# Linear attention and two feed-forward layers on one core: the attention's normalisation moved to tokens on partitions, the first block's loads rebuilt, and a new model of the queues in the planner

## The chip, the cores and the metric

One core of one Trainium2 chip runs the whole program. Times are device microseconds (us). The kernel before takes 1663.95 us, the median of three runs (1659.26 to 1665.63).

## The reference

Everything is float32.

```
kv  = einsum('bhsd,bhse->bhde', k, v)          # 8 batches, 8 heads, 576 tokens, 64 wide
out = einsum('bhsd,bhde->bhse', q, kv)
x   = out / sqrt(mean(out*out, -1) + 1e-6) * g_norm      # per head; then 4608 tokens x 512
h = x @ w_in;   g = s * relu(h)**2 + b;   x = g @ w_out      # 512 -> 2048 -> 512
h = x @ w_in2;  g = h * cos(h);           out = g @ w_out2
```

The weights arrive as float64, so each tile of them is first converted: two 32-bit words are turned into one float32 by two ScalarE and four VectorE operations (function w_conv, lines 313 to 366).

## The kernel before

**How a product is computed.** A float32 matmul is either "native" (one instruction of two passes for each product, lines 672 and 518) or "split": each operand is kept as a rounded part and a remainder (hi, lo), and three single-pass products (hi hi, hi lo, lo hi) are summed in PSUM (lines 629 to 631 and 680). Splitting an operand costs one ScalarE copy and one VectorE subtraction.

**Stages.** The 4608 tokens are nine blocks of 512. Blocks 0 to 2 go through the first layer in 48 steps (a block has 16 slices f of the hidden width; step i is block i // 16, slice i % 16). Step i computes h (mm_h, line 621, twelve passes of 512 columns), activates it (act1, line 640) and adds to four accumulators (mm_o, line 665). In block 0 the steps that are in WHOLE, all 16, use the unsplit w_out and native matmuls (line 672); while block 1 runs, split_late (line 383) splits these w_out tiles for the later steps. Blocks 3 to 8 and the whole second layer are done afterwards in 80 pairs of slices with a Strassen-like scheme (mm_h2, line 809, act2, act1_pair, mm_o1). The trace has the first instruction of these pairs at 389 us.

**Attention.** attn_unit (line 538) makes x for one block and one pair of heads: four units for each block. Where a new batch begins, kv_unit (line 486) loads k and v as four rows per partition on 128 partitions (512 tokens, 1 KB packets) and the last 64 tokens as "tails" on 64 partitions (256 B packets), in four DMAs (lines 497 and 500; for blocks 2 and up from POOL's queue), and multiplies them in ten matmuls (line 518). q is brought with its width on partitions: in block 0 by four TensorE transposes (line 551), else by 128 B packets and a VectorE transpose (line 572). Then xps = kv.T q, 512 tokens along the free axis (line 582); the mean of squares over a head lies along partitions, so it is a matmul with a matrix of 1/64 (line 588 native in block 0; else the squares are split, lines 591 and 592, and two passes are made, lines 596 and 597). The inverse root is refined by one Newton step on 128x512 tiles: two ScalarE operations (602, 604) and three VectorE operations (606, 608, 610). For blocks 0 to 2 the result is split (532, 533); for the others it is stored to memory (615).

**Order.** The order on every engine is worked out beforehand by class Plan (lines 61 to 159). Each op has an engine, a cost and a due time; the planner runs a clock for each engine, takes the op that can start first, and among those within 0.1 us the one due first. SP, SUM (POOL's queue) and AQ (ScalarE's queue) are such engines too; after an op its users wait for AFTER (0.13 to 0.2 us for compute, 2.0, 4.5 and 3.0 us for the three queues). On the chip each engine runs its list in that order and waits where the model was too early. warm_up (line 904) adds 40 matmuls of the identity that fill TensorE where the plan finds nothing else.

**Block 0's loads** (load_block0, line 464): two w_in tiles go first on ScalarE's queue (line 319); SP takes k and v of the first head pair, both tails, q in 256 B packets (line 473), the constants (line 285), then the other head pairs and the other weights.

Of the kernel before, what the change touches and what calls it, by code (L numbers as in the profile page):

```python
# [10 lines left out]
F32 = mybir.dt.float32  # L11
# [29 lines left out]
FIRST_LOADS = {0: -39.6, 1: -38.7, 2: -37.6, 3: -36.8}  # L41
WARM = 40

WHOLE = range(16)
# [16 lines left out]
class Plan:  # L61
# [7 lines left out]
    AFTER = {"PE": 0.2, "DVE": 0.13, "ACT": 0.13, "POOL": 0.13, "SP": 2.0, "SUM": 4.5, "AQ": 3.0}  # L69
# [6 lines left out]
    def op(self, eng, cost, due, fn, w=(), p=(), r=(), keep=(), after=()):  # L76

# [25 lines left out]
    def run(self):  # L103
        engines = dict(self.START)
        ready = {e: [] for e in self.AFTER}
# [13 lines left out]
        def start(o):  # L119
            t = max(engines[o.eng], o.ready)  # L120
            for x in o.refs:
                if x.slots and x.t is None:
                    t = max(t, min(free_at(s) for s in x.slots))
            return t

        n = 0
        while n < len(self.ops):
# [13 lines left out]
            end = t + o.cost  # L141
            engines[o.eng] = end
# [7 lines left out]
            for x in o.refs:  # L150
                x.left -= 1
                x.end = max(x.end, end)
                if not x.left and x.slots:
                    hold(x.slot, x.end + self.AFTER[o.eng])
            for u in o.users:
                u.ready = max(u.ready, end + (0.0 if u.eng == o.eng == "PE" else self.AFTER[o.eng]))
# [6 lines left out]
def fused_kernel(  # L163
# [27 lines left out]
    R = S // P  # L191
    TAIL = S - R * P
# [62 lines left out]
    EARLY = {"kv_raw", *Q_RAW, *TAIL_, *KV_F, *QT, *QH, *QL}  # L255
# [14 lines left out]
    ones = cpool.tile([P, P], F32R, name="ones")  # L270
    nc.vector.memset(f32(ones), 0.0)
    for j in range(2):

        nc.vector.memset(f32(ones)[j * D:(j + 1) * D, j * D:(j + 1) * D], 1.0 / D)
# [4 lines left out]
    small = cpool.tile([P, 5], F32, name="small")  # L279
    g_sb, g_neg, s_sb, b_sb, spare = (small[:, i:i + 1] for i in range(5))  # L280
    g_ref, sb_ref = Ref(), Ref()

    def load_consts():
        for j in range(2):
            op("SP", 0.5, -39.5, lambda j=j: nc.sync.dma_start(
                out=g_sb[j * D:(j + 1) * D, :], in_=g_norm.rearrange("(p o) -> p o", o=1)), p=[g_ref])
        op("DVE", 0.1, -30, lambda: nc.vector.tensor_scalar(
            out=g_neg, in0=g_sb, scalar1=-1.0, scalar2=None, op0=ALU.mult), w=[g_ref])
        for t, src in ((s_sb, moe_s), (b_sb, moe_b)):
            op("SP", 0.5, -30, lambda t=t, src=src: nc.sync.dma_start(  # L290
# [22 lines left out]
    def w_conv(ph, kind, f, by, load_by=None, after=()):  # L313
# [5 lines left out]
        early = ph == 0 and kind == "i" and f < 2  # L319
        queue = nc.scalar if early else nc.sync  # L320
# [18 lines left out]
        op("AQ" if early else "SP", 1.0 if early else 1.5, by - 12 if load_by is None else load_by, load, w=[raw], after=after)  # L339

        op("ACT", 0.67, by - 6, lambda: nc.scalar.activation(t.t, w1().bitcast(F32), AF.Abs), w=[t], r=[raw])  # L341
        op("DVE", 0.43, by - 5, lambda: nc.vector.tensor_scalar(
            out=t.t, in0=t.t, scalar1=F64_HI, scalar2=F64_LO, op0=ALU.min, op1=ALU.max), w=[t])
        op("DVE", 0.43, by - 5, lambda: nc.vector.tensor_scalar(
            out=ti(), in0=ti(), scalar1=3, scalar2=0x3FFFFFFF, op0=ALU.logical_shift_left, op1=ALU.bitwise_and),
            w=[t])
        op("DVE", 0.69, by - 4.5, lambda: nc.vector.scalar_tensor_tensor(
# [3 lines left out]
        op("ACT", 0.67, by - 4.5, lambda: nc.scalar.activation(w0(), w0().bitcast(U32), AF.Copy, scale=2.0 ** -29),  # L351
           w=[raw])
        if ph == 0 and kind == "o" and f in WHOLE:

            op("DVE", 0.69, by - 3, lambda: nc.vector.tensor_tensor(out=w0(), in0=ti(), in1=w0(), op=ALU.add),
# [3 lines left out]
        op("DVE", 0.69, by - 3, lambda: nc.vector.tensor_tensor(out=ti(), in0=ti(), in1=w0(), op=ALU.add),  # L359
# [11 lines left out]
    def split_in(kind, f, t, by):  # L371

        hi = w_t[0, kind, f] = sref([(WO if kind == "o" else WI)[f]], F32R, (2, 512))
        op("ACT", 0.62, by - 1, lambda: nc.scalar.copy(hi.t[:, 0, :], t.t), w=[hi], r=[t])
# [89 lines left out]
    def load_block0():  # L464
# [17 lines left out]
        for hp in range(1, KC):  # L482
            load_kv(hp, -40 + hp)
            load_q(hp, -40 + hp)
# [545 lines left out]
```

## Time and profile before

| | |
|---|---|
| runs | 1665.63, 1659.26, 1663.95 us; median 1663.95 |
| profiled execution, from first to last instruction | 1660.2 us |
| what lies around that span | not given for the profiled execution; the median of the runs is 3.75 us above its span |
| TensorE busy | 1634.8 us (98%) |
| VectorE, ScalarE, GpSimd busy | 1136.9, 916.9, 86.3 us |
| weight loads on TensorE | 1424.3 us (86%) |
| mean granted TensorE clock | 0.996 of full speed |

TensorE is busy nearly all the time, so what counts is where it is not, and where what it does is a filler (line 910) or more passes than needed. A row of a window gives busy time (and instructions, x) of each engine, then the granted TensorE clock, the busy share of the DMA engines and what they moved in GB/s. In a timeline a row is: start, length, engine, line, operation, output <- input, shape, count, and in brackets the idle time before it with what ended that. Ends of matmuls are modelled: the time of a group is read from its start to the next start.

### The profile page before, as it was taken

The page shows a single profiled execution, that of the slowest core. Times are in us where ns is not written, and L with a number is a line of the kernel's source. Part 1 is how long each engine was busy: PE and PEld are TensorE (multiplying, and loading weights), DVE is VectorE, ACT ScalarE, POOL GpSimd, SP SyncE. Part 2 cuts the span into 40 slices and gives each one's busy share as a digit, 9 for nine tenths or more (in the row PEclk, how much of TensorE's full clock was granted, in tenths as well). Part 3 has the DMA queues.
Part 4 walks back from the last instruction along what each step waited for, and adds up shares of the span by engine and source line. Part 5 has one row for each costly group of instructions (what it writes and reads, how often), then busy time and mean ns, then how long its engine had stood idle before and what let it go on. Part 6 is the DMA issues. An engine that isn't in the chain of part 4 may idle for free.

```text
span 1660.2 us, 23829 instructions
## 1 busy us (share of the span) xinstructions
PE 1634.8 (98%) x8648; PEld 1424.3 (86%) x8648; DVE 1136.9 (68%) x1804; ACT 916.9 (55%) x1551; POOL 86.3 (5%) x142
## 2 busy tenths in 40 slices
PE   8999999999999999999999999999999999999999
PEld 6666776778989989988999998998998998988987
DVE  6897787785667767767346567567567577577564
ACT  6775765454556556556335455555555555455443
POOL 0012443300000000000000000000000000000000
PEclk9999999999999999999999999999999999999999
DMA  9733788944678777876565543443443444444431
GB/s 304 210 99 93 204 226 213 267 144 128 234 227 270 251 247 242 262 252 198 184 220 197 172 153 124 153 155 121 151 160 120 149 158 125 148 156 128 147 116 55
DMA packets 207446, 297.29 MB, mean 179 GB/s; under 512 B 89313, under 2 KB 134369, under 8 KB 207329
## 3 DMA queue, kind: packets, MB, share of 16 engines
q1 hardware_dynamic: 198848, 274.26, 53.1%
q0 software_dynamic: 7424, 20.46, 4.2%
q8 instruction: 69, 1.13, 0.3%
q10 hardware_dynamic: 1056, 1.05, 0.2%
q14 instruction: 49, 0.39, 0.1%
HBM read 232.79 MB, written 62.91 MB: 178 GB/s over the span
## 4 chain that ended last, share of the span: by engine, by line
PE 55%; DMA 1%; ACT 0%; issue 0%; DVE 0%; SPq 0%; ACTq 0%; DVEq 0%
PE h L823 25%; PE a L680 16%; PE h L680 8%; PE a L718 4%; PE h L718 2%; DMA w2i_d<-t 0%; DMA raw<-in_moe_w_out_dram 0%; DMA raw<-in_moe_w_in_dram 0%; ACT t L835 0%; ACT c L341 0%; ACT wi L896 0%; ACT wi L893 0%; DVE t L396 0%; ACT t L395 0%; ACT t L698 0%
## 5 line engine op out<-in xcount | busy, mean ns | idle before, releaser
L823 PE MATMUL h<-shared,wi 128*128 128x384 f32 x2256 | 466.9, 337 | 3.2 <-ACT t L835 3.2
L823 PEld LDWEIGHTS h<-shared,wi 128*128 128x128 f32 x2256 | 400.5, 188 | 15.8 <-ACT t L835 4.2
L680 PE MATMUL a<-wo,wi 128*128 128x512 f32 x964 | 258.6, 391 | 0.0
L835 ACT COPY t<-h 128x384 f32<-128x384 f32 x233 | 111.4, 479 | 225.6 <-PE h L823 217.4
L680 PEld LDWEIGHTS a<-wo,wi 128*128 128x128 f32 x964 | 180.0, 188 | 33.5
L718 PE MATMUL a<-wi,wo 128*128 128x256 f32 (+1 forms) x1152 | 203.3, 317 | 0.0
L718 PEld LDWEIGHTS a<-wi,wo 128*128 128x128 f32 x1152 | 178.1, 188 | 18.3 <-DVE t L729 0.4
L680 PE MATMUL h<-wo,wi 128*128 128x512 f32 x482 | 130.1, 392 | 0.0
L877 ACT ACTIVATE wi<-wi 128x768 f32<-128x768 f32 x96 | 81.5, 849 | 78.6 <-DVE wi L875 78.6
L823 PE MATMUL h<-late,wi 128*128 128x384 f32 x528 | 120.2, 336 | 0.7 <-ACT t L835 0.7
L823 PE MATMUL h<-g,wi 128*128 128x384 f32 x504 | 114.2, 337 | 1.7 <-ACT t L835 1.5
L869 ACT ACTIVATE wi<-wi 128x768 f32<-128x768 f32 x95 | 80.6, 849 | 47.3 <-DVE wi L839 45.3
L680 PEld LDWEIGHTS h<-wo,wi 128*128 128x128 f32 x482 | 89.8, 188 | 15.9
L839 DVE TENSOR_TENSOR wi<-h,t 128x384 f32<-128x384 f32 x125 | 69.5, 556 | 49.1 <-PE h L823 38.2
L718 PE MATMUL h<-wi,wo 128*128 128x512 f32 x384 | 100.7, 394 | 0.8 <-DVE wi L898 0.8
L680 PE MATMUL a<-g,wo 128*128 128x512 f32 x384 | 99.4, 399 | 0.0
L823 PEld LDWEIGHTS h<-late,wi 128*128 128x128 f32 x528 | 94.1, 188 | 6.0 <-ACT t L835 1.1
L823 PEld LDWEIGHTS h<-g,wi 128*128 128x128 f32 x504 | 89.1, 188 | 6.0 <-ACT t L835 1.9
L873 DVE SCALAR_TENSOR_TENSOR wi<-wi,wi 128x768 f32<-128x768 f32 x95 | 90.7, 955 | 1.7
L879 DVE TENSOR_TENSOR wi<-wi,wi 128x768 f32<-128x768 f32 x95 | 90.6, 954 | 1.7 <-ACT wi L877 0.2
L871 DVE TENSOR_SCALAR wi<-wi 128x768 f32<-128x768 f32 x96 | 53.7, 559 | 47.4 <-ACT wi L869 45.1
L629 PE MATMUL h<-shared,wi 128*128 128x512 f32 x192 | 85.0, 443 | 1.1 <-DVE t L610 1.0
(182 smaller groups left out, 2550.9 us busy)
## 6 DMA issues: line engine op xcount, KB each, us to landing
wi<-w2i_d SPq DMA_DIRECT2D x144, 512.0 KB, 4.3
wi<-w1i_d SPq DMA_DIRECT2D x96, 512.0 KB, 4.7
late<-x_d SPq DMA_DIRECT2D x36, 384.0 KB, 6.3
w2i_d<-t SPq DMA_DIRECT2D x48, 256.0 KB, 4.3
wi<-w2i_d SPq DMA_DIRECT2D x48, 256.0 KB, 2.7
x_d<-t SPq DMA_DIRECT2D x40, 256.0 KB, 2.8
wo<-in_moe_w_out_dram SPq DMA_DIRECT2D x16, 512.0 KB, 6.9
w1i_d<-t SPq DMA_DIRECT2D x32, 256.0 KB, 3.7
```

What stands on the lines that cost most here:

```text
L629: nc.tensor.matmul(h.t, wh, hi, start=(c == 0), stop=False)
L680: nc.tensor.matmul(o.t, a, b, start=(first and z == 0), stop=(last and z == 2))
L718: nc.tensor.matmul(dst, x[:, sl], y[:, src], start=(first and z == i == 0), stop=(last and z == 2), skip_group_check=a >= 4)
L823: nc.tensor.matmul(o.t[:, 0:HT], a, b, start=(first and c == z == 0), stop=(c == 1 and z == 2), skip_group_check=not first)
L835: op("ACT", 0.52, by + 1, lambda: nc.scalar.copy(dst(), o.t[:, 0:HT]), p=[s], r=[o])
L839: op("DVE", 0.57, by + 1, lambda: nc.vector.tensor_tensor(out=h[f].t[:, half * HT:(half + 1) * HT], in0=a.t[:, 0:HT], in1=s.t, op=ALU.add) ...
L869: op("ACT", act, by, lambda u=u, x=x: nc.scalar.activation(u.t, x.t, AF.Identity, scale=1.0 / TWO_PI, bias=0.25), w=[u], r=[x])
L871: op("DVE", two, by + 1, lambda u=u: nc.vector.tensor_scalar(out=u.t, in0=u.t, scalar1=MAGIC, scalar2=-MAGIC, op0=ALU.add, op1=ALU.add), w ...
L873: op("DVE", one, by + 2, lambda u=u, x=x: nc.vector.scalar_tensor_tensor(out=u.t, in0=x.t, scalar=1.0 / TWO_PI, in1=u.t, op0=ALU.mult, op1 ...
L877: op("ACT", act, by + 4, lambda u=u: nc.scalar.activation(u.t, u.t, AF.Sin, scale=TWO_PI, bias=0.5 * math.pi), w=[u])
L879: op("DVE", one, by + 5, lambda u=u, x=x: nc.vector.tensor_tensor(out=u.t, in0=u.t, in1=x.t, op=ALU.mult), w=[u], r=[x])
```

## The change

The mean of squares is taken with tokens on partitions: xps is now q.T kv in pieces of at most 128 tokens, the sum over a head's 64 columns is a VectorE reduction, the Newton step runs on 128x8 numbers, and the scaled result is transposed back by four TensorE transposes; g_norm is applied by the last ScalarE or VectorE operation. k and v are loaded as six rows on each of 96 partitions (1.5 KB packets, no tails), each into a tile of its own (three tiles instead of two that hold both). In block 0 attention's loads stand first on SP, q (1 KB packets) of the first two head pairs goes on ScalarE's queue, the constants on POOL's, and w_in tiles follow; tiles for q come from more buffers. Slices 12 to 15 of block 0 are split (WHOLE is now range(12)). The planner issues a DMA in 0.4 to 0.72 us, models one shared DMA pipe behind the queues, and has compute costs nearer to the durations, times 1.0 or 1.14. Cost numbers of all other ops were replaced likewise.

```
-FIRST_LOADS = {0: -39.6, 1: -38.7, 2: -37.6, 3: -36.8}
+FIRST_LOADS = {0: -39.5, 1: -37.5, 2: -36.5, 3: -36.4}
-WHOLE = range(16)
+WHOLE = range(12)
...
-    AFTER = {"PE": 0.2, "DVE": 0.13, "ACT": 0.13, "POOL": 0.13, "SP": 2.0, "SUM": 4.5, "AQ": 3.0}
+    AFTER = {"PE": 0.2, "DVE": 0.13, "ACT": 0.14, "POOL": 0.13}
+    ISSUE = {"SP": 0.4, "SUM": 0.72, "AQ": 0.5}
+    TO_DMA, LANDS = 1.4, 0.5
+    SLACK = {"PE": 1.0, "DVE": 1.14, "ACT": 1.14, "POOL": 1.0}
+    BUSY = 1.3
...
-            end = t + o.cost
-            engines[o.eng] = end
+            if o.eng in self.ISSUE:
+                engines[o.eng] = t + self.ISSUE[o.eng]
+                dma = max(dma, t + self.TO_DMA) + o.cost * self.BUSY
+                end = seen = dma + self.LANDS
+            else:
+                end = engines[o.eng] = t + o.cost * self.SLACK[o.eng]
+                seen = end + self.AFTER[o.eng]
...
-    KV_RAW, Q_RAW, TAIL_ = ["kv_raw", "raw"], ["q_raw", "q_raw1"], ["tail", "tail1"]
+    KV_RAW, Q_RAW = ["kv_raw", "kv_raw1", "raw"], ["q_raw", "q_raw1"]
-    QT, QH, QL = ["qT", "qT1"], ["qh"], ["ql"]
+    QT, AT, SM = ["qT", "qT1"], slots("at", 3), slots("sm", 4)
...
     def load_consts():
-            op("SP", 0.5, -39.5, lambda j=j: nc.sync.dma_start(
+            op("SUM", 0.02, -39.5, lambda j=j: nc.gpsimd.dma_start(
...
-        early = ph == 0 and kind == "i" and f < 2
-        queue = nc.scalar if early else nc.sync
+        queue = nc.sync
...
+    def kv_load(queue, t, src, b, h0):
+        queue.dma_start(
+            out=t.t[0:KP, 0:2 * R * D].rearrange("p (h r d) -> p h r d", h=2, r=R),
+            in_=src[b, h0:h0 + 2].rearrange("h (p r) d -> p h r d", r=R))
...
         def load_q(n, by):
+            op("AQ" if n < 2 else "SP", 0.75, by, lambda: (nc.scalar if n < 2 else nc.sync).dma_start(
+                out=q0[n].t.rearrange("p (h c d) -> p h c d", h=2, c=KC),
+                in_=q[0, 2 * n:2 * n + 2, 0:TB, :].rearrange("h (p c) d -> p h c d", c=KC)), p=[q0[n]])
+        for hp in range(KC):
             load_kv(hp, -40 + hp)
             load_q(hp, -40 + hp)
...
-            k_t = v_t = sref(KV_RAW, F32, (1024,))
+            k_t, v_t = (sref(KV_RAW, F32, (2 * R * D,)) for i in range(2))
...
-            for r in range(R + 1):
+            for r in range(R):
...
             def transpose():
                 for c in range(KC):
-                    nc.tensor.transpose(
-                        ps.t[:, c * P:(c + 1) * P], q0[hp].t[:, 0, c, :], ident
-                    )
+                    for h in range(2):
+                        at = (h * KC + c) * D
+                        nc.tensor.matmul(
+                            ps.t.rearrange("p (t c) -> p c t", c=KC)[h * D:(h + 1) * D, c, :],
+                            q0[hp].t[:, at:at + D], ident, start=True, stop=True)
...
         def mm_x():
-                nc.tensor.matmul(xps.t[:, sl], kvt.t, qT.t[:, sl], start=True, stop=True)
+            for b, t0, n in pieces(j):
+                c, p0 = divmod(t0, P)
+                nc.tensor.matmul(xps.t[p0:p0 + n, c * P:(c + 1) * P], qT.t[:, t0:t0 + n], kvs[b].t,
+                                 start=True, stop=True)
...
         op("ACT", 0.495, by - 7, lambda: nc.scalar.activation(sq.t, xps.t, AF.Square), w=[sq], r=[xps])
+        op("DVE", 0.6, by - 6, lambda: nc.vector.tensor_reduce(
+            out=ss(), in_=heads(sq.t), axis=mybir.AxisListType.X, op=ALU.add), w=[sm], r=[sq])
+        op("ACT", 0.2, by - 5, lambda: nc.scalar.activation(
+            r0(), ss(), AF.Abs_reciprocal_sqrt, scale=1.0 / D, bias=EPS), w=[sm])
...
+        op("DVE", 0.66, by - 5, lambda: nc.vector.tensor_tensor(
+            out=heads(xn.t), in0=heads(xps.t), in1=rs().unsqueeze(2).to_broadcast([P, 2 * KC, D]), op=ALU.mult),
+            w=[xn], r=[xps, sm])
+        op("PE", 0.45, by - 3, transpose_x, w=[xT], r=[xn])
+        if j < NE:
+            op("ACT", 0.5, by - 1, lambda: nc.scalar.activation(x.t[:, 0], xT.t, AF.Identity, scale=g_sb),
+            op("DVE", 0.66, by, lambda: nc.vector.scalar_tensor_tensor(
+                out=x.t[:, 1], in0=xT.t, scalar=g_sb, in1=f32(x.t[:, 0]), op0=ALU.mult, op1=ALU.subtract),
         else:
+            op("ACT", 0.5, by - 1, lambda: nc.scalar.activation(a.t, xT.t, AF.Identity, scale=g_sb),
```

The four small VectorE operations of the Newton step (128x8) stand between the root and the last product. pieces(j) cuts a block's 512 tokens at multiples of 128 and where a batch ends: four pieces in even blocks, five in blocks 1, 3, 5 and 7.

## Rows read from the trace of the kernel before

**Rows 1.** The page: span and TensorE's busy time.
```profile
span 1660.2 us, 23829 instructions
PE 1634.8 (98%) x8648; PEld 1424.3 (86%) x8648; DVE 1136.9 (68%) x1804; ACT 916.9 (55%) x1551; POOL 86.3 (5%) x142
```

**Rows 2.** Stretches: PE, PEld, DVE, ACT, POOL busy; clock; DMA share; GB/s.
```profile
0.00:8.00 8.00, 5.75 (x38) 5.34 (x38) 1.24 (x5) 2.15 (x3) 1.85 (x14) 1.00 0.80 229
8.00:10.00 2.00, 0.00 (x0) 0.00 (x0) 0.87 (x2) 0.66 (x1) 0.00 (x0) 0.96 1.25 131
10.00:16.00 6.00, 5.55 (x22) 4.24 (x22) 3.33 (x7) 3.10 (x6) 0.00 (x0) 0.50 0.88 256
16.00:28.00 12.00, 11.95 (x100) 7.88 (x100) 7.03 (x12) 10.78 (x22) 0.00 (x0) 0.97 1.04 322
28.00:42.60 14.60, 14.52 (x76) 11.52 (x75) 14.19 (x28) 12.19 (x22) 0.00 (x0) 1.00 1.07 370
...
100.00:150.00 50.00, 50.00 (x221) 31.59 (x220) 37.55 (x69) 30.60 (x57) 11.17 (x18) 1.00 0.29 70
150.00:350.00 200.00, 189.72 (x1143) 144.67 (x1141) 157.00 (x258) 123.09 (x245) 71.08 (x108) 0.99 0.82 218
...
450.00:800.00 350.00, 343.56 (x1957) 318.84 (x1956) 248.34 (x411) 202.68 (x345) 0.00 (x0) 1.00 0.75 242
```

**Rows 3.** Timeline of TensorE's matmuls in the first 50 us.
```profile
10.45 0.48 PE L518 MATMUL a<-wo 64*64 64x64 f32 x4 [3.03 <-DMA wo<-in_v_dram]
...
25.91 0.47 PE L629 MATMUL h<-shared,wi 128*128 128x512 f32 x1
...
33.83 1.95 PE L910 MATMUL h<-ident 128*128 128x128 f32 x16
35.53 0.48 PE L629 MATMUL h<-shared,wi 128*128 128x512 f32 x1
...
42.62 3.59 PE L672 MATMUL a<-g,wo 128*128 128x512 f32 x8
```

**Rows 4.** Timeline of SP's queue: the issue of q and of g_norm.
```profile
3.53 1.36 SPq L473 DMA_DIRECT2D wi<-in_q_dram  x2
5.83 2.83 SPq L285 DMA_DIRECT2D small<-in_g_norm_dram  x2
```

**Rows 5.** Groups of instructions, 100 to 350 us; the last row from the tile `small`.
```profile
L610 DVE SCALAR_TENSOR_TENSOR t<-h,small,t 128x512 f32<-128x512 f32 x28 | 20.9, 747 | 0.2
L606 DVE SCALAR_TENSOR_TENSOR t<-h,t 128x512 f32<-128x512 f32 x28 | 19.2, 686 | 11.5 <-ACT t L604 11.3
L656 ACT ACTIVATE g<-t,small 128x512 fp32r<-128x512 f32 x24 | 17.3, 720 | 3.0 <-DVE t L644 2.9
L287 DVE TENSOR_SCALAR small<-small x1: 155/155/155, 11.4 to 11.4; 128x1 f32<-128x1 f32 x1
```

**Rows 6.** Timeline of TensorE: a split step's products with w_out.
```profile
157.35 2.88 PE L680 MATMUL a<-g,wo 128*128 128x512 f32 x12
```

**Rows 7.** Timeline of TensorE: attention's products (k and v; a transposed q).
```profile
25.05 0.66 PE L551 MATMUL h<-ident,wi 128*128 128x128 f32 x4
25.54 0.61 PE L910 MATMUL h<-ident 128*128 128x128 f32 x4
...
71.65 0.69 PE L518 MATMUL h<-kv_raw 128*64 128x64 f32 x16
72.26 0.33 PE L518 MATMUL h<-tail 64*64 64x64 f32 x4
72.53 0.50 PE L629 MATMUL h<-shared,wi 128*128 128x512 f32 x1
```

**Rows 8.** Waits, 150 to 350 us: who waited for whom, total, times, longest.
```profile
PE h L597 <- DVE ql L592: 2.6, 1, 2.6
DVE t L396 <- DMA w1i_d<-t: 5.6, 2, 4.1
```

**Rows 9.** Line 497, the loads of k and v: time from issue to landing.
```profile
DMA to landing us min/median/max: 3.1/4.4/10.8
```

More of the change, by code (lines that the diff above doesn't have):

```diff
@@ L119, in start @@
         def start(o):
-            t = max(engines[o.eng], o.ready)
+            t, taken = max(engines[o.eng], o.ready), []
             for x in o.refs:
                 if x.slots and x.t is None:
-                    t = max(t, min(free_at(s) for s in x.slots))
+                    first, slot = min((free_at(s) if s not in taken else 1e9, s) for s in x.slots)
+                    t = max(t, first)
+                    taken.append(slot)
             return t
@@ L278, in fused_kernel @@
         op("POOL", 0.2, -99, lambda t=t: nc.gpsimd.memset(t.t, 0.0), w=[t])
-    small = cpool.tile([P, 5], F32, name="small")
-    g_sb, g_neg, s_sb, b_sb, spare = (small[:, i:i + 1] for i in range(5))
+    small = cpool.tile([P, 4], F32, name="small")
+    g_sb, s_sb, b_sb, spare = (small[:, i:i + 1] for i in range(4))
     g_ref, sb_ref = Ref(), Ref()
@@ L403, in store @@
                 nc.sync.dma_start(out=d, in_=src)
-            op("SP", 0.8, by, store, p=[ref], r=[part])
+            op("SP", n * 0.0013, by, store, p=[ref], r=[part])
     def w_sums(u, tu, tv, by, whole_ones=True):
@@ L518, in mm, with pieces @@
                     nc.tensor.matmul(
-                        ps.t[sl, sl], rows(k_t, 0, h, r), rows(v_t, 1, h, r), start=(r == 0), stop=(r == R)
+                        ps.t[sl, sl], rows(k_t, h, r), rows(v_t, h, r), start=(r == 0), stop=(r == R - 1)
                     )
-        op("PE", 0.85, by - 4, mm, w=[ps], r=[k_t, v_t, tail], after=tf.readers)
+        op("PE", 0.78, by - 4, mm, w=[ps], r=[k_t, v_t], after=tf.readers)
         for h in range(2):
             sl = slice(h * D, (h + 1) * D)
-            op("ACT", 0.12, by - 3, lambda sl=sl: nc.scalar.copy(tf.t[sl, sl], ps.t[sl, sl]), p=[tf], r=[ps])
+            op("ACT", 0.21, by - 3, lambda sl=sl: nc.scalar.copy(tf.t[sl, sl], ps.t[sl, sl]), p=[tf], r=[ps])
     xs = {}
-    def split_x(j, c, t, by):
-        x = xs[j, c] = sref(X[c], F32R, (2, TB))
-        op("ACT", 0.62, by, lambda: nc.scalar.copy(x.t[:, 0], t.t), w=[x], r=[t])
-        op("DVE", 0.69, by, lambda: nc.vector.tensor_tensor(
-            out=x.t[:, 1], in0=t.t, in1=f32(x.t[:, 0]), op=ALU.subtract), w=[x], r=[t])
-    ms_ops, x_ops = [], []
+    x_ops = []
+    def pieces(j):
+        return [(b, max(off, c * P), min(off + n, c * P + P) - max(off, c * P))
+                for off, n, b, s in segments(j) for c in range(KC) if off < c * P + P and off + n > c * P]
     def attn_unit(j, hp, by, after=()):
@@ L573, in attn_unit @@
                after=x_ops[-1:])
-        kvs = [kv_f[b % 2, hp] for off, n, b, s in segs]
+        kvs = {b: kv_f[b % 2, hp] for off, n, b, s in segs}
         xps = pref([*ACC[1:3], *HB3] if j == 0 else HB3 + HB1 if j > 1 else HB3)
-        sq = sref(T)
-        ms = pref(ACC[3:] if j == 0 else HB2)
+        sq, xn = (sref([*AT, *T] if native else AT) for z in range(2))
+        xT = pref([ACC[3], ACC[0]] if j == 0 else HB2)
+        sm = sref(SM, F32, (4, 2 * KC))
         def mm_x():
-            for (off, n, b, s), kvt in zip(segs, kvs):
-                sl = slice(off, off + n)
-                nc.tensor.matmul(xps.t[:, sl], kvt.t, qT.t[:, sl], start=True, stop=True)
@@ new lines, in heads @@
+        def heads(t):
+            return t.rearrange("p (a e) -> p a e", e=D)
+        ss, r0, u, rs = (lambda i=i: sm.t[:, i, :] for i in range(4))
+        x_ops.append(op("PE", 0.88 + 0.15 * (len(pieces(j)) - KC), by - 8, mm_x, w=[xps], r=[qT, *kvs.values()]))
+        op("ACT", 0.495, by - 7, lambda: nc.scalar.activation(sq.t, xps.t, AF.Square), w=[sq], r=[xps])
+        op("DVE", 0.6, by - 6, lambda: nc.vector.tensor_reduce(
+            out=ss(), in_=heads(sq.t), axis=mybir.AxisListType.X, op=ALU.add), w=[sm], r=[sq])
@@ L863, in act2 @@
         g = {}
-        one, two, act = 0.96, 0.56, 0.84
+        one, two, act = 0.88, 0.47, 0.75
         for f, by in ((1, pair_due(n + 1)), (0, pair_due(n + 1) + 2)):
```

209 lines of the change are left out of this document (83 added, 126 removed).

## The prediction

> **What bounds the kernel now.** I read the page first: in a span of 1660.2 us TensorE is busy 1634.8 [rows 1]. More work for VectorE, ScalarE or the queues costs nothing by itself; what counts is TensorE's passes, and the stretches in which it waits or fills. The view by stretches then says where these lie [rows 2]: from 150 to 350 us TensorE is busy 189.72 of 200, so 10.3 us are idle there; from 450 to 800 it is 343.56 of 350, 6.4 idle; from 100 to 150 nothing. The head looks full and is not: 80 filler instructions of line 910 are in it, and in its timeline the first pass of the first layer starts at 25.91 and the first product with w_out at 42.62 [rows 3]. From there TensorE has no gap till 150.
>
> In the head the reader should see two different limits [rows 2]. Until 28 us data and chains limit: VectorE is busy 1.24, 0.87, 3.33 and 7.03, in all 12.5 of 28. From 28 to 42.6 VectorE is busy 14.19 of 14.6, so it is the engine that ends last there; the fillers at 33.83 (1.7 us to the next start) wait for it [rows 3]. Up to 42.6 VectorE works 26.7 us and idles 15.9. The early loss is visible too: the tail of k and v ends a TensorE wait of 3.03 us at 10.45 [rows 3]; from 8 to 10 us the DMA engines are busy throughout (share 1.25) but move 131 GB/s, against 229 before and 256 after [rows 2], which is when the 256 B packets of tails and q are under way; and after that idle stretch the granted clock is 0.50, the 1.2 GHz level, from 10 to 16 us.
>
> **The change part by part.** The sum is made against the profiled span, 1660.2; the runs' median lies 3.75 above it, and I add that at the end.
>
> *Block 0's loads.* Ahead of the first unit's chain stood two w_in tiles (1.05 MB), the first k and v, all tails and the first q. Now it is the first k and v (0.59 MB) and q of two pairs (0.52), then w_in. With the 229 GB/s of the first 8 us [rows 2], 1.11 MB take 4.8 us and with w_in 0 (0.52 MB) 7.2. All of attention's data and two w_in tiles are 4.46 MB: 1.83 in the first 8 us, the rest at 322 GB/s in 8.2 us, so they are in at about 16. SP no longer spends 2.83 us on g_norm [rows 4]. VectorE's work up to the first product with w_out stays: of each unit four 128x512 operations become three of that size and four small ones; with 686 ns for the reduction (the nearest row, an operation of the same size), 747 each for the product and the remainder that read PSUM, and 155 for a small one, it is 2.8 us against 2.8 (686, 686, 747, 686) [rows 5]. So 26.7 us of VectorE work have to fit in after the data come. If VectorE first has work at 7.5 us and idles another 3 to 4 up to the dense part (it idled 8.8 of the 20 us from 8 to 28 [rows 2]; I allow it under half of that), its idle time is 11 instead of 15.9: **5 us less**. Upper bound of the gain: no idle after 6.5 us, 9 us. Lower bound: conversions come as late as before, because w_in now stands behind attention on SP: nothing. I take 5, in the middle, since attention's own chain is what VectorE lacked. The change of queue is not in this sum; it is one of several loads in flight: q was issued at 3.53 to 4.89 [rows 4] and can now be issued at once.
>
> From 16 to 42.6 us, when SP alone issues, the DMA engines' share is 1.04 and 1.07 [rows 2], so a second queue finds no room there; what it could add lies before. The Trainium skill, DMA: Bandwidth & Descriptors, "Issuing engines are not separate DMA queues", has a rule that speaks against the part with the queues: several issuing engines save only the sequencer's time. By it that part alone is worth at most the 3 us by which q is issued sooner, 3 instead of 5; the sum above rests on order and bytes.
>
> *Slices 12 to 15 split.* A native step's products with w_out are eight instructions of 3.59 us [rows 3], a split one's are twelve of 2.88 [rows 6]: 0.71 less, four times, **2.8 us less** on TensorE. It adds 0.69 + 0.75 us of VectorE for each (the tile's and the activation's remainder), 5.8 us in the part from 100 to 150 us, where VectorE is busy 37.55 of 50 [rows 2]; that cover holds. If it were gone the steps would take VectorE's time and nothing would be gained, so the bounds are 0 and 2.8. The later splitting of these four tiles goes away from the stretch after 150.
>
> *Attention on TensorE, blocks 1 to 8.* Units: 32, of which 28 have a k and v product.
> - k and v: 16 instructions of full rows take 0.61 us and the four of the tail 0.27 [rows 7], where 4/16 of 0.61 would be 0.15; so 0.12 is the change of row count. Six row groups at 0.153 are 0.92 against 0.88, or 0.80 if the 0.61 also holds an end: -0.08 to +0.04, times 28: -2.2 to +1.1. I take 0.
> - the mean of squares: two passes at a twelfth of 2.88 [rows 6], 0.48, go; four transposes come, 0.49 by the four at 25.05 [rows 7]. Nothing.
> - xps: 512 columns in two passes either way; a piece of 128 has two passes of 0.12 [rows 7]. The fifth piece in the odd blocks costs up to two more, 0.24, in 16 units: 0 (if the two half pieces, which write different partitions, run side by side) to 3.9. I take **2 us more**.
>
> What the trace shows here is 0.12 us lost where instructions of 64 rows follow those of 128 [rows 7]. The Trainium skill, TensorEngine Tiling (Array Packing), "Key Properties", has it as a rule against this change: a switch of tiling mode drains the engine. By the rule, five-piece units, which go to half-width pieces and back, would pay two such drains, 0.24 in 16 units or 3.9 us, while 28 units save one at the tail, 3.4 us; the sum would be 0.5 instead of 2.
>
> *Attention elsewhere.* VectorE saves the squares' remainder and one Newton operation: for each unit 5 or 6 operations of about 0.69 become 3 or 4 and four small ones (0.62), 0.75 us less; 24 units from 150 to 350 give 18 of its 157 us [rows 2]. ScalarE loses two 128x512 operations and gains a small one. Two tiles of T are no longer taken by each unit, and T is where VectorE waited 5.6 us for a store [rows 8]. The 2.6 us that TensorE waits for the squares' remainder [rows 8] has no successor of that form, but a new one: the four transposes stand behind Square, reduction, root, four small operations and the product, about 3.4 us by the same rows, and whatever is queued behind them on TensorE (the next step's passes) waits if VectorE is late. Of the 10.3 us idle I take half away: **5 us less**, between 10.3 less and 3 more (the new wait hits about as often as the old one). If these stalls go, the next to be late is k and v (below).
>
> *The planner.* It changes the order everywhere, also in the pairs of slices, whose 6.4 us of idle time from 450 to 800 hang on loads and stores. Compute costs there stay near the old ones (0.88 times 1.14 for 0.96); the loads' model is new. Nothing to 6.4 less or the like more; I take **1.5 less**, as the model now counts transfers that share the engines. The rest of the span (800 on) is dense and stays.
>
> Sum: -5 - 2.8 + 2 - 5 - 1.5 = -12.3; the span becomes 1647.9 and the time **1651.7**.
>
> **The rivals.**
> 1. *The head does not move and the stalls only change place.* VectorE is full from 28 on [rows 2], and w_in tiles now arrive later; if the conversions and not attention decide, the 5 us stay, and the new transposes stall as the squares did. Left: -2.8 + 2 - 2 = -3, about 1661: no change that can be measured. For it: VectorE's 14.19 of 14.6. Against: 8.8 idle us just before that.
> 2. *Most of the idle time goes.* A head 9 us shorter, 9 us of the stalls, 4 in the pairs, the split steps: -25 with nothing added on TensorE, 1639. For it: all three have one cause, planned times that differ from real ones. Against: the dense planner order may bring others.
> 3. *Slower: k and v come too late.* k and v now share three tiles, so v of a unit can be loaded only after the products of the unit before it; landing takes 4.4 us, up to 10.8 [rows 9], while the plan counts on a shortest time of 3.1 (1.4, 0.95 times 1.3, 0.5) for POOL's queue where it counted 5.7. TensorE runs in order, so its first layer waits behind the product. If 24 units wait 1.3 us (4.4 less 3.1), that is 31 us more; head, split steps, pairs and the added passes still give -7.3, so +24, about 1688. It decides (over 8.3 us slower) from 0.65 us a unit on. For it: the DMA share of 0.82 from 150 to 350. Against: the new model lets transfers queue behind each other, which lengthens the planned time exactly when the share is high.
> 4. That the change does not do what it says has little room: the diff shows the matmuls, loads and tiles.
>
> **How the numbers follow.** My case 0.6, with a range of its own of 1643 to 1660 (the bounds of the head and of the stalls, one of them at its end at a time); rival 1 0.21, rival 2 0.12, rival 3 0.07. The predicted time is that of the likeliest case. A measurement of this kernel tells about 0.5% from no change: 8.3 us, so faster means below 1655.6, slower above 1672.3. My case lies below 1655.6 with about 0.9 of its chance and else in between; rival 2 is faster; rival 1 is the same. That gives 0.66 faster (0.54 + 0.12), 0.27 the same (0.06 + 0.21), 0.07 slower. The range goes from rival 2's 1638 to rival 1's upper end, 1664.
>
> **What would show it.** In the changed profile the first w_out product should start near 37 instead of 42.62, VectorE should be busier before 28 us, and the wait for a tail and the stretch of 131 GB/s should be gone. The products of four more steps in block 0 should be of 12 instructions. From 150 to 350 TensorE should be idle about 5 us. A row of TensorE waiting for k or v loads with many times speaks for rival 3; waits for the product before the transposes, as large as the 10.3 us, for rival 1. I am wrong if the head's dense part starts within 1 us of 42.6, or if TensorE's busy time without fillers grows.

## The result, and the profile after

The changed kernel takes **1645.83 us** (median of 4 runs, 1644.66 to 1646.41), the kernel before beside it 1664.47; the ratio is 0.9901 [0.9885, 0.9917]. The profiled execution has a span of 1643.8 us, 16.4 less than before. The page's first rows, which answer to [rows 1]:

```profile
span 1643.8 us, 24612 instructions
PE 1632.6 (99%) x9104; PEld 1438.8 (88%) x9104; DVE 1114.2 (68%) x1880; ACT 876.6 (53%) x1503; POOL 55.6 (3%) x98
```

The stretches of the changed kernel, with the columns of [rows 2]:

```profile
0.00:8.00 8.00, 5.38 (x40) 4.95 (x40) 0.00 (x0) 2.07 (x3) 4.14 (x18) 1.00 0.75 222
8.00:10.00 2.00, 2.00 (x28) 1.58 (x26) 0.00 (x0) 0.58 (x1) 0.00 (x0) 1.00 0.53 163
10.00:16.00 6.00, 6.00 (x79) 5.67 (x75) 3.89 (x10) 2.91 (x8) 0.00 (x0) 1.00 1.09 276
16.00:28.00 12.00, 12.00 (x150) 11.11 (x149) 8.83 (x23) 8.28 (x19) 0.00 (x0) 1.00 1.09 331
28.00:42.60 14.60, 13.41 (x56) 9.13 (x55) 14.48 (x31) 12.40 (x23) 0.00 (x0) 1.00 1.06 376
...
150.00:350.00 200.00, 200.00 (x1416) 161.84 (x1415) 138.74 (x296) 94.88 (x205) 45.98 (x72) 1.00 0.81 219
...
450.00:800.00 350.00, 348.54 (x1986) 323.21 (x1985) 244.71 (x400) 200.93 (x342) 0.00 (x0) 1.00 0.74 241
```

From 150 to 350 us TensorE no longer idles at all (10.3 us before), from 450 to 800 it idles 1.5 (6.4 before). The clock stays at 1.00 in the head, where [rows 2] had a stretch at 0.50 behind the wait for the tail; that wait and the 131 GB/s are gone. All that TensorE still waits for by name:

```profile
PE h L822 <- ACT t L834: 1.8, 2, 1.1
PE h L909 <- POOL ident masks.py:199: 1.4, 1, 1.4
PE h L544 <- DMA wi<-in_q_dram: 1.2, 1, 1.2
PE h L628 <- ACT shared L605: 0.8, 1, 0.8
PE h L717 <- DVE wi L897: 0.8, 1, 0.8
PE h L629 <- DVE shared L607: 0.3, 1, 0.3
```

No row names a load of k or v, and none the product ahead of the four transposes. The timeline of TensorE in the changed kernel's head, against [rows 3]:

```profile
23.04 1.05 PE L544 MATMUL h<-ident,wi 128*64 128x128 f32 x16
24.01 0.50 PE L628 MATMUL h<-shared,wi 128*128 128x512 f32 x1
...
38.97 3.59 PE L671 MATMUL a<-g,wo 128*128 128x512 f32 x8
...
44.48 3.60 PE L671 MATMUL a<-g,wo 128*128 128x512 f32 x8
```

The first product with w_out comes 3.65 us earlier, but with 13 triples of the first layer (a triple is the three passes hi hi, hi lo, lo hi) ahead of it, where the kernel before has 14. The second product has 16 triples ahead of it in both and comes 2.96 us earlier. In the kernel before it stands at:

```profile
47.44 3.59 PE L672 MATMUL a<-g,wo 128*128 128x512 f32 x8
```

**Where the 16.4 us went** (for TensorE's classes: from each pass's start to the next one's, less idle time, summed over the trace; "behind the head" is from the first product with w_out on):

| part | forecast | found |
|---|---|---|
| head, to the first product with w_out | -5 | -3.65 |
| four steps split (4 x 0.76, below) | -2.8 | -3.0 |
| attention on TensorE, behind the head | +2 | +1.5 |
| idle, 150 to 350 us | -5 | -10.3 |
| idle, 450 to 800 us | -1.5 | -5.0 |
| idle, 400 to 450 us (0 before) | 0 | +1.2 |
| 1656 w_out passes in the pairs, 1.25 ns each more | 0 | +2.1 |
| all else behind the head | 0 | +0.7 |

The sum of the last column is -16.45. In "all else" are the triple that moved behind the head (0.7) and the time behind TensorE's last pass (0.9 more). Seen the other way, TensorE is busy 1634.8 us before and 1632.6 after, of which its 80 fillers take 12.99 and 10.67 from start to start. That leaves 1621.8 and 1621.9 us. The products take as long as before; idle time and fillers went.

### The profile page after: what moved, and what is told of

Read it like the earlier page. It is cut to its first block, busy times and chain, and to the rows that moved or that the text cites. A ratio compares the mean times of both kernels' runs of the same rounds, so it can differ in the third digit from the quotient of the medians.

```text
span 1643.8 us, 24612 instructions
## 1 busy us (share of the span) xinstructions
PE 1632.6 (99%) x9104; PEld 1438.8 (88%) x9104; DVE 1114.2 (68%) x1880; ACT 876.6 (53%) x1503; POOL 55.6 (3%) x98
## 4 chain that ended last, share of the span: by engine, by line
PE 96%; DMA 2%; DVE 1%; ACT 0%; issue 0%; SPq 0%; ACTq 0%; DVEq 0%
PE h L822 35%; PE a L679 22%; PE a L717 10%; PE h L679 8%; PE h L717 5%; PE h L628 3%; PE h L630 3%; PE h L629 3%; PE a L671 3%; PE h L575 2%; PE h L510 2%; DMA raw<-in_moe_w_out_dram 1%; PE h L600 1%; DMA w2i_d<-t 0%; DMA raw<-in_moe_w_in_dram 0%; PE h L909 0%
## 5 line engine op out<-in xcount | busy, mean ns | idle before, releaser
L822 PE MATMUL h<-shared,wi 128*128 128x384 f32 x2232 | 446.3, 336 | 0.1
L822 PEld LDWEIGHTS h<-shared,wi 128*128 128x128 f32 x2232 | 393.7, 188 | 14.0 <-ACT t L834 1.0
L679 PE MATMUL a<-g,wo 128*128 128x512 f32 x432 | 112.6, 399 | 0.0
L822 PE MATMUL h<-late,wi 128*128 128x384 f32 x552 | 111.4, 335 | 0.0
L822 PE MATMUL h<-g,wi 128*128 128x384 f32 x504 | 110.2, 337 | 0.7 <-ACT t L834 0.7
L679 PEld LDWEIGHTS h<-wo,wi 128*128 128x128 f32 x482 | 90.0, 188 | 16.4
L679 PEld LDWEIGHTS a<-g,wo 128*128 128x128 f32 x432 | 78.5, 188 | 16.1 <-issue 0.3
## 6 DMA issues: line engine op xcount, KB each, us to landing
wi<-in_moe_w_in_dram SPq DMA_DIRECT2D x16, 512.0 KB, 10.4
```

The costliest lines, as they stand in the source:

```text
L679: nc.tensor.matmul(o.t, a, b, start=(first and z == 0), stop=(last and z == 2))
L822: nc.tensor.matmul(o.t[:, 0:HT], a, b, start=(first and c == z == 0), stop=(c == 1 and z == 2), skip_group_check=not first)
```

## The experiments

Each ran beside the kernel before (median 1662.68 to 1664.51 us) on one chip, not all on the same one, so kernels are compared by ratio. By the intervals, two ratios closer than about 0.0025 (4 us, an estimate) are not told apart. "Idle" is TensorE's, 200 or 350 us less its busy time. The next column is the start of the first product with w_out, with the number of triples ahead of it in brackets. The last is the mean time from start to start, less idle time, of the same 1656 w_out passes in the pairs (those of the second layer without the last 72).

| kernel | us | ratio | idle 150:350, 450:800 | first w_out | ns |
|---|---|---|---|---|---|
| before | 1664.47 | 1 | 10.3, 6.4 | 42.62 (14) | 229.4 |
| changed | 1645.83 | 0.9901 [0.9885, 0.9917] | 0, 1.5 | 38.97 (13) | 230.6 |
| after_again | 1647.29 | 0.9905 [0.9886, 0.9924] | 0, 1.1 | 39.35 (13) | 230.6 |
| planner_only | 1650.71 | 0.9924 [0.9897, 0.9952] | 5.4, 2.0 | 41.70 (14) | 229.0 |
| planner_loads | 1648.49 | 0.9903 [0.9885, 0.992] | 5.7, 2.6 | 40.41 (14) | 229.2 |
| planner_12 | 1644.31 | 0.9884 [0.9866, 0.9902] | 2.3, 2.8 | 40.71 (14) | 229.0 |
| loads_12 | 1649.45 | 0.9908 [0.9888, 0.9927] | 2.2, 6.3 | 40.88 (14) | 229.2 |
| old_planner | 1669.91 | 1.0038 [1.0021, 1.0054] | 11.9, 6.2 | 42.48 (12) | 230.4 |
| whole16 | 1654.21 | 0.9952 [0.9935, 0.9968] | 2.8, 2.0 | 39.55 (13) | 230.6 |
| whole8 | 1648.33 | 0.9911 [0.9893, 0.9929] | 0, 3.0 | 40.19 (13) | 231.1 |
| four_pieces | 1642.28 | 0.9876 [0.9852, 0.99] | 0, 3.3 | 39.50 (13) | 231.0 |
| w_in_first | 1643.53 | 0.9884 [0.9868, 0.9899] | 0, 1.4 | 42.92 (13) | 229.0 |
| one_queue | 1648.69 | 0.9916 [0.99, 0.9932] | 0.2, 2.0 | 40.21 (13) | 231.6 |
| w_in_on_act | 1646.63 | 0.9902 [0.9884, 0.9919] | 0.5, 2.6 | 44.91 (13) | 229.0 |

One execution's head is good to about a microsecond: after_again, whole16, whole8 and four_pieces run the changed kernel's head in the same order on every engine, and in the five the first product starts at 38.97 to 40.19 us. Between kernels with different numbers of triples, the second product (16 ahead in all) tells more: 47.44 before, 44.48 in the changed kernel (44.48 to 45.70 in the five, 45.01 in the middle), 46.52 in planner_only, 45.53 in planner_12, 48.67 in old_planner.

**Planner or normalisation?** planner_only is the kernel before with the planner's new model and all its new costs:

```
+    ISSUE = {"SP": 0.4, "SUM": 0.72, "AQ": 0.5}
+    TO_DMA, LANDS = 1.4, 0.5
...
-            end = t + o.cost
+                dma = max(dma, t + self.TO_DMA) + o.cost * self.BUSY
```

> The kernel before with the new planner and its cost numbers alone; attention, block 0's loads and the split steps are as before. If the lighter normalisation took the idle time away, TensorE still idles about 10 us from 150 to 350 us and the time is 1657 to 1664 us. If the planner did it (its times for loads and for compute come nearer to the real ones), TensorE idles under 3 us there, about 5 us of the 6.4 us from 450 to 800 us go as well, and the time is about 1648 to 1652 us. The head's first product with w_out stays near 42.6 us under both.

old_planner is its counterpart: the changed kernel, with the planner and the costs outside attention and block 0 as before.

```
-                dma = max(dma, t + self.TO_DMA) + o.cost * self.BUSY
...
+            end = t + o.cost
```

> The changed kernel with the planner and all compute and load costs of before outside attention and block 0. If the normalisation took the idle time away, TensorE idles under 3 us from 150 to 350 us and the time is 1646 to 1652 us. If the planner did it, about 10 us of idle time come back there and some 5 us from 450 to 800 us, and the time is 1656 to 1662 us.

The planner alone gives 13 us (8 to 17 by its interval); the rest without the planner is 0.4% slower than the kernel before, and slower than either of its theories. planner_only's time is what the planner's theory asked for, its stalls are not: 5.4 us stay from 150 to 350, where under 3 were expected. The stretch from 150 to 350 us in old_planner, and then its largest waits (whole execution):

```profile
150.00:350.00 200.00, 188.08 (x1401) 151.49 (x1398) 132.26 (x298) 94.61 (x208) 48.22 (x75) 0.97 0.80 217
```

```profile
PE h L585 <- ACT kvf L503: 6.5, 2, 3.9
PE h L807 <- ACT t L819: 5.4, 6, 1.6
PE h L585 <- DVE at L579: 3.7, 3, 1.4
PE h L495 <- DMA wo<-in_v_dram: 3.0, 2, 1.7
```

Line 585 is the four transposes: TensorE stands at them 3.7 us for VectorE's product (line 579), the new wait of the prediction's rival 1 at about a third of the size it named (10.3). Another 6.5 us are for ScalarE's copy of k and v's product (line 503), which has to empty the PSUM tile that the transposes write. The longest of these waits, in TensorE's timeline, and what ScalarE did before that copy:

```profile
298.03 1.12 PE L585 MATMUL h<-ident,at 128*128 128x128 f32 x4 [3.91 <-ACT kvf L503]
```

```profile
296.58 0.59 ACT L682 COPY c<-a 128x512 f32<-128x512 f32 x1 [6.40 <-DMA x_d<-c]
```

ScalarE was not busy: it stood 6.40 us at an eviction whose buffer was still being stored. That store was issued at 289.98 and landed 6.5 us later, with the DMA engines at a share of 1.05 from 290 to 298 us. VectorE is busy 25 us less in this stretch than in [rows 2], and TensorE idles more: the lighter load by itself did not shorten the waits, and the longest of them came from the order of loads and stores. One rival is left for the 3.7 us: old_planner plans the new normalisation without the factor 1.14 (0.6 us for the reduction, which takes 0.69), so its VectorE work is late against the plan; that was not tried by itself. Under the new planner and with the split steps, the same normalisation leaves no idle time.

planner_12 adds the split steps to planner_only and nothing else.

```
-WHOLE = range(16)
+WHOLE = range(12)
```

> The kernel before with the new planner and its new costs, and with slices 12 to 15 split from block 0 on; attention, its loads and block 0 are those of before. It answers what the new normalisation and the new loads are worth once planner and split steps are given. Theory: the split steps are worth about 8 us by themselves (all 16 native cost 8.4 us in the changed kernel), so from 1650.7 this goes to about 1643, 2 to 3 us below the changed kernel's 1645.8: the normalisation with tokens on partitions then gives nothing and costs some 3 us (five pieces). Rival A: the split steps are worth what was forecast, 2.8 us: 1648. Rival B: the split steps only pay with the new normalisation, because the old one's VectorE work fills 100 to 150 us: 1650 or more, with a TensorE wait for VectorE there.

1644.31, as good as the changed kernel within the intervals: given planner and split steps, the normalisation and the rebuilt loads are worth nothing that these runs can tell. The old normalisation keeps 2.3 us idle from 150 to 350; the new kernel pays for its fifth pieces, and 2.7 us for the wider spacing in the last column.

planner_loads is planner_only with the compute costs of before on VectorE and ScalarE (but for three in act2, which stay new); the model of loads and of free buffers, and the loads' costs, stay.

```
-    SLACK = {"PE": 1.0, "DVE": 1.14, "ACT": 1.14, "POOL": 1.0}
+    SLACK = {"PE": 1.0, "DVE": 1.0, "ACT": 1.0, "POOL": 1.0}
...
-        op("DVE", 0.6, by, lambda: nc.vector.tensor_tensor(
+        op("DVE", 0.69, by, lambda: nc.vector.tensor_tensor(
```

> The kernel before with the new planner's model of the loads and of free buffers alone (issue times, shared transfer time, landing); the compute costs and their factor stay as before. With both, the time was 1650.7. Theory: compute costs hardly change (0.6 times 1.14 is 0.684 where 0.69 stood), so the model of the loads carries the gain: 1649 to 1653. Rival: the order follows the compute costs (evictions of ScalarE and the small k and v copies changed most), and the loads were never late: 1659 to 1664.

The theory held: that model carries the gain. planner_loads, with nothing else of the change, stands level with the whole of it (0.9903 against 0.9901 and 0.9905). Which part of the model does it (issue times, the shared transfer time, landing, free buffers, the loads' costs) was not tried. loads_12, planner_loads with planner_12's one line, was to beat the changed kernel.

> The kernel before with two parts of the change alone: the planner's model of the loads and of free buffers, and slices 12 to 15 split from block 0 on. Compute costs, attention, its loads and block 0 are those of before. Theory (these two parts are the whole gain, and add): the model of the loads gave 1648.5, the split steps 6.4 behind the full planner (1650.7 to 1644.3), so 1641 to 1644, below the changed kernel's 1645.8 to 1647.3. Rival (the split steps need the new compute costs, or the normalisation's lighter VectorE work): 1646 or more, no better than the changed kernel.

It didn't: the rival held. Its first stretches do gain (2.2 idle instead of 5.7), and the pairs give it back. Its stretch, and its largest wait:

```profile
450.00:800.00 350.00, 343.66 (x1956) 318.69 (x1956) 243.44 (x399) 200.78 (x341) 0.00 (x0) 1.00 0.74 238
```

```profile
PE h L838 <- ACT t L850: 5.0, 7, 1.5
```

The pairs wait for ScalarE's evictions (line 850). Its old cost (0.52 us, against 0.38 times 1.14 in the changed plan) may be why, but planner_loads has the same cost and idles 2.6 there; that was not tried by itself. What is shown is that parts which each gain in their own stretch need not add, since every edit reorders what follows.

**What a split step is worth.** whole16 is the changed kernel with all steps native again, whole8 has four more split.

```
-WHOLE = range(12)
+WHOLE = range(16)
```

> The changed kernel with all 16 steps of block 0 native again. If the split steps gain what TensorE's passes say, 0.71 us for each of four, the time is 2 to 3 us longer, about 1648.5 us. If VectorE's added work in these steps had eaten the gain, there is no difference or a gain, 1644 to 1646 us.

> The changed kernel with slices 8 to 15 split from block 0 on instead of 12 to 15. Theory: the four steps that went from native to split gave 8.4 us; four more give as much as long as VectorE has room in the steps concerned, which it has less of (about 50.8 of the 57.4 us from 42.6 to 100 are busy): 1638 to 1643. Rival (VectorE binds there): a TensorE wait for VectorE in the part from 60 to 110 us takes the gain back, 1645 to 1652.

TensorE's timeline of the same step in whole16, a native one, and in the changed kernel, a split one (start, us, line, count):

```profile
123.81 3.60 PE L671 MATMUL a<-g,wo 128*128 128x512 f32 x8
126.84 0.79 PE L628 MATMUL h<-shared,wi 128*128 128x512 f32 x1
127.48 0.39 PE L629 MATMUL h<-shared,wi 128*128 128x512 f32 x1
...
130.01 3.59 PE L671 MATMUL a<-g,wo 128*128 128x512 f32 x8
```

```profile
125.27 2.88 PE L679 MATMUL a<-g,wo 128*128 128x512 f32 x12
127.99 0.39 PE L628 MATMUL h<-shared,wi 128*128 128x512 f32 x1
128.21 0.39 PE L629 MATMUL h<-shared,wi 128*128 128x512 f32 x1
...
130.71 2.88 PE L679 MATMUL a<-g,wo 128*128 128x512 f32 x12
```

The native step lasts 6.20 us, the split one 5.44: 0.76 less, 3.0 for four. Start to start the products themselves differ by 0.31 (3.03 against 2.72); the other 0.4 lies behind them, where the first pass of the first layer's next product takes 0.64 to the next start instead of 0.22. But whole16 is 8.4 us slower, its span 6.6 longer. Its waits name 2.4 us more:

```profile
PE h L510 <- ACT t L612: 1.5, 1, 1.5
PE h L510 <- DVE shared L607: 0.9, 1, 0.9
```

Line 510 is k and v's product: behind 150 us it waits for ScalarE and VectorE (idle 2.8 there, against 0). They then have four more tiles to split, till 245 us instead of 209; that this makes them late is argued, not tried by itself. With half a us of a later head, which is scatter, that makes 6.3 of the 6.6. whole8 misses its theory: it is no faster than the changed kernel. Of this the head's 1.2 us are scatter too; the pairs idle 1.5 more, and from 100 to 150 us TensorE idles 2.2, of which two waits of line 600 (the transposes) for VectorE make 1.9. So VectorE does bind there, though mildly, as the rival said.

**The fifth piece.** four_pieces takes four pieces in the odd blocks too; it leaves out that a piece may hold tokens of two batches (some tokens take the wrong batch's k and v).

```
-        return [(b, max(off, c * P), min(off + n, c * P + P) - max(off, c * P))
+        return [(next(b ... if off <= c * P < off + n), c * P, P) for c in range(KC)]
```

> The changed kernel with four pieces for the product of q and kv in every block; it leaves out that in the odd blocks some tokens of one piece belong to another batch, and multiplies them by the first batch's kv. If the fifth piece costs its two passes and the change of width, about 0.31 us a unit in 16 units, 5 us go: about 1641 us, and a group of this product is 0.81 us in all blocks. If the two half pieces run side by side and cost nothing, the time stays at 1645 to 1647 us.

The passes of x shrink from 35.16 to 30.44 us, 4.7 less, and the time falls by 3.6 against the changed kernel, at the edge of what the intervals tell. In the changed kernel's timeline a unit of five pieces and one of four:

```profile
100.35 1.26 PE L575 MATMUL h<-kvf,qT 128*64 128x128 f32 x10
101.44 0.60 PE L600 MATMUL h<-ident,at 128*128 128x128 f32 x4
...
144.02 1.05 PE L575 MATMUL h<-kvf,qT 128*128 128x128 f32 x8
144.83 0.48 PE L628 MATMUL h<-shared,wi 128*128 128x512 f32 x1
```

Start to start 1.09 and 0.81 here (1.14 in the mean of the sixteen): ten passes cost 0.28 to 0.33 more than eight, and at 0.10 a pass 0.2 of that are the passes. The rest speaks for the rule of the Trainium skill, TensorEngine Tiling (Array Packing), "Key Properties" (a change of tiling mode drains the engine), at 0.04 to 0.07 us a change rather than the 0.12 that was worked out for it.

**The head.** w_in_first lets two w_in tiles lead again on ScalarE's queue, with q on SP:

```
-FIRST_LOADS = {0: -39.5, 1: -37.5, 2: -36.5, 3: -36.4}
+FIRST_LOADS = {0: -41.0, 1: -40.9, 2: -36.5, 3: -36.4}
...
+        early = ph == 0 and kind == "i" and f < 2
+        queue = nc.scalar if early else nc.sync
```

one_queue puts q and the constants on SP:

```
-            op("AQ" if n < 2 else "SP", 0.75, by, lambda: (nc.scalar if n < 2 else nc.sync).dma_start(
+            op("SP", 0.75, by, lambda: nc.sync.dma_start(
```

w_in_on_act has the `early` lines of w_in_first and nothing else, so that the first q leads on ScalarE's queue; the plan then puts a w_in tile ahead of the second.

> The changed kernel, but the first two w_in tiles lead again on ScalarE's queue, and q is issued on SP behind k and v. It undoes the order of the first loads and nothing else of block 0. Theory (order and bytes give the head's gain): 1.05 MB at about 222 GB/s stand ahead of attention's, so VectorE's first operation starts later and the first product with w_out moves from 38.97 toward 42.6: 2 to 4 us more, 1648 to 1650. Rival (the head is set by VectorE's work, and the conversions of the two w_in tiles fill the start): no later than now, 1644 to 1646.

> The changed kernel with the constants and the first two q loads on SP's queue instead of GpSimd's and ScalarE's: only the queues are undone, the packets and the order by bytes stay. By the rule of the Trainium skill weighed in the prediction (several issuing engines save only the sequencer's time) it costs the issue time that SP then spends, about 2 to 3 us at the start of the chain and less at its end: first product with w_out at 39.5 to 41, time 1646 to 1648. Rival (the queues themselves carry the gain): first product with w_out at 42 or later, 1649 or more.

> The changed kernel with only the queue of the first two w_in tiles undone: they go on ScalarE's queue behind the first two q, so attention's loads still lead. Theory (the w_in tiles on ScalarE's queue go with the closer spacing, the order of the loads with the early head): first product with w_out near 39 and 227 ns in the pairs, 1641 to 1643. Rival (spacing goes with the order, or with neither): 231 ns and 1645 to 1647.

The first w_out product starts at 42.92, 40.21 and 44.91, against 38.97. So the order of the first loads, with the queues of q and w_in that change with it, is worth 2.7 to 3.95 us of the head by the five equal ones. The queues of q and the constants alone are worth no more than the scatter: one_queue's head, 1.24 us later, is as late as the latest of the five. Nothing there speaks against the Trainium skill, DMA: Bandwidth & Descriptors, "Issuing engines are not separate DMA queues" (several issuing engines save only the sequencer's time). In w_in_on_act the queue decides all the same. The timeline of its head:

```profile
12.15 1.98 PE L545 MATMUL h<-ident,wi 128*64 128x128 f32 x16 [2.34 <-DMA wi<-in_q_dram]
```

The second q, issued at 1.75 us behind one w_in tile on ScalarE's queue, lands 10.4 us after its issue and is waited for till 12.15. In the changed kernel it was issued at 1.22 with nothing but the first q ahead, landed 5.1 us later and was in use by 8.4. On that queue the loads landed in the order of their issue in both (4.72, 8.94 and 12.10 us here), so what stands ahead of a load on its own queue counts, not only what is in flight.

All three miss the times expected: one_queue by 0.7 us, less than the intervals tell, w_in_on_act by its late head, and w_in_first, which was to take 1648 to 1650, takes 1643.53, no slower than the changed kernel. The 3.95 us lost in the head come back behind it, 4.3 us in all, of which 2.7 are in the last column of the table. In TensorE's timeline, an uninterrupted group of twelve in the changed kernel, then in w_in_first:

```profile
919.61 2.97 PE L679 MATMUL a<-wo,wi 128*128 128x512 f32 x12
922.42 1.52 PE L679 MATMUL h<-wo,wi 128*128 128x512 f32 x6
```

```profile
922.34 2.88 PE L680 MATMUL a<-wo,wi 128*128 128x512 f32 x12
925.06 1.30 PE L680 MATMUL h<-wo,wi 128*128 128x512 f32 x5
```

2.81 us against 2.72 for the same twelve passes, with no wait in either and the clock at 1.00. after_again, the changed kernel unchanged, was run to see whether that is chance.

> The changed kernel once more, unchanged, beside the others on one chip. It answers whether the spacing of the uninterrupted w_out passes in the pairs (231 ns at the median in the changed kernel, 227 ns in the kernel before and in the one with the two w_in tiles first) belongs to the kernel or to the one execution that was profiled. Theory: to the kernel, 231 again and 1645 to 1647. Rival: to the execution, about 227 or something else.

It isn't: 230.6 ns again. In the table the kernels whose first two w_in tiles go on ScalarE's queue have 229.0 to 229.4, all others 230.4 to 231.6. w_in_on_act shows the same step for an edit of that queue alone. It is not the order of what runs then: from 50 us on, all engines and SP's queue run the same list in the same order in w_in_on_act and in the changed kernel. Whether buffers or code lie elsewhere in memory was not looked at. Why the placement of two loads in the first 3 us should change the spacing of passes 900 us later was not found.

## Why the prediction was right, and where it was not

The time lies in the range, 5.9 us below the forecast, on the side that was given the most chance. For the mechanism that is in good part luck. Of the 12.3 us forecast, 10.8 were laid on block 0's loads, the split steps and the normalisation and 1.5 on the planner. In the runs the planner's model of the loads reaches the same time alone (planner_loads, 1648.49). Loads, split steps and normalisation without it take 0.4% more than the kernel before (old_planner). Point by point:

1. **Head**, -5 forecast, -3.65 found, 2.96 of it at equal work (2.4 with the middle one of five equal heads): the size is near, the step is wrong. It said that VectorE's 26.7 us of work stay and that its idle time falls from 15.9 to 11. The two heads, up to the first product with w_out, before and after:

```profile
0.00:42.62 42.62, 37.79 (x234) 28.97 (x235) 26.69 (x51) 28.90 (x53) 1.85 (x14) 0.92 0.99 303
```

```profile
0.00:38.97 38.97, 35.17 (x328) 30.70 (x329) 23.57 (x55) 22.71 (x47) 4.14 (x18) 1.00 0.98 304
```

   VectorE idles 15.9 and 15.4; its work fell by 3.1. Two of these are conversions that ran ahead of need before (lines 342 and 344 seven times each, now lines 349 and 351 six and five), 0.5 the memsets and the constant that went. Its first operation comes at 11.62, not at 7.5: attention's first chain has none of VectorE's work until x is normalised, and w_in now lands later. Before 28 us VectorE is hardly busier (12.7 against 12.5), which was to show the step. Nor is all of it block 0's: planner_12, with the old loads, has the second product with w_out at 45.53, so 1.9 us come with the planner and the split steps, most of the 2.4 to 2.96. Under the old planner the new loads bring it no earlier than before (48.67). Both figures are of one execution each.
2. **Split steps**: the term was right, 2.8 forecast and 3.0 measured, though it was read from modelled lengths (3.59 and 2.88). From start to start the products differ by 0.31 a step; the 0.4 behind them, which the prediction did not have, makes up for it. Its cover was not what was said: "the later splitting goes away from the stretch after 150" stood at nothing, and whole16 shows some 3 us of waits there.
3. **Attention on TensorE**: the sum held (+1.5), by terms that cancel. Over the whole kernel the fifth piece was sized at 2 and measured 4.7; eight narrow passes for two wide ones, held equal, cost 2.3; transposes for the mean of squares, held equal, save 5.8 (15.0 against 20.8); k and v save 2.2; and block 0's q now takes 16 transposes a unit instead of 4, 3.3 us in the head that no step named.
4. **Stalls** 150 to 350: half was taken, all of it went. The cause given was VectorE's lighter load; old_planner (11.9 idle with it) and planner_12 (2.3 without it) refute it as the cause by itself. The planner takes about half alone (5.4 left), with the split steps more (2.3 left, planner_12), with the normalisation but no split steps as much (2.8 left, whole16); only all three leave nothing.
5. **Planner**: mis-sized. It was given 1.5 us, in the pairs alone; it is worth 13 us by itself, in head, stalls and pairs, and its model of the loads alone is worth as much.

Of the rivals, 3 (k and v late) has no row in the changed kernel's waits; the new wait of 1 exists in old_planner (3.7 us) and whole8 (1.9), not in the changed kernel; 2 came nearest, with most of the idle time gone and a smaller head. Its reason, one cause for all three, planned times that differ from real ones, is what the runs bear out. Of the two signs of being wrong neither came: the head starts 3.65 us from 42.6, and TensorE's busy time without fillers is unchanged. Two of the prediction's figures are a little off: 0.24 in 16 units is 3.8 us, and rival 2 ends at 1639.

## What to carry to other kernels

Where TensorE is 98% busy and the rest is idle time at changing places, price the change of the schedule first: here a new model of the loads was worth as much as the whole change. Test a lighter normalisation, or any relief of an engine off the bound, under the old order and the new one; VectorE lost 25 of 157 us in one stretch and TensorE waited longer. And compare long passages of identical work between two kernels: 1.6 ns on each of 1656 passes hid 2.7 us of a 4 us loss. And before a difference of a microsecond in one trace's head is called an effect, look at a second execution of the same head: five of them here span 1.2 us.

## What the runs showed of the hardware that was not expected

- A split pass takes 229.0 to 229.4 or 230.4 to 231.6 ns in the mean. Which of the two goes with the queue of the kernel's first w_in loads, and two executions of one kernel agree (230.6); the cause is open.
- A native fp32 product costs more behind it than in it: 0.31 us of the step's 0.76 are its own passes, the first pass after it takes 0.4 longer.
- A transposed q as sixteen passes "128*64" takes 0.97 us (23.04 to 24.01 in the changed kernel), where four passes 128*128 took 0.49 [rows 7].
